# One block of p*v per pair of tiles, and a new timetable for the next pair's preparation and for the weight conversions, in a fused attention, MoE and SwiGLU kernel

## Chip, core and metric

The kernel runs on one core of one Trainium2 chip. The metric is the device time of one execution in microseconds (us); lower is better. The kernel before takes 814.34 us, the median of three runs (813.39 to 814.79).

## What is computed

The reference chains three parts. The part that the change touches is the first, an attention in which a query only sees keys of its own hash bucket:

```python
def _attn_ref(q, k, v, proj):             # q, k, v: (2, 8, 768, 64), proj: (64, 6)
    q_bits = (np.einsum('bhsd,dk->bhsk', q, proj) > 0).astype(np.int64)
    k_bits = (np.einsum('bhsd,dk->bhsk', k, proj) > 0).astype(np.int64)
    powers = 2 ** np.arange(n_bits)
    mask = (q_bits * powers).sum(-1)[:, :, :, None] == (k_bits * powers).sum(-1)[:, :, None, :]
    scores = np.where(mask, scale * np.matmul(q, k.transpose(0, 1, 3, 2)), -1000000000.0)
    attn = np.exp(scores - scores.max(-1, keepdims=True))
    attn = attn / (attn.sum(-1, keepdims=True) + 1e-09)
    return np.matmul(attn, v).astype(np.float32)
```

Its output (1536 tokens of 512) goes through a mixture of 8 experts with 192 tokens each, and then through a normalised SwiGLU layer whose three weights arrive as 64-bit floats.

## The kernel before, in words

**Units.** Heads are worked in pairs: 2 batches by 4 pairs of heads are 8 pairs, numbered p. A pair has 6 tiles of 128 queries, and a tile has two heads, so a pair is 12 *units*, and the main loop (L601) runs over 96 units u. A unit is one head of one tile of 128 queries against all 768 keys. The place of a unit within its pair, 0 to 11, is called its slot here; slot -1 is the last unit of the pair before.

**What a unit issues.** The order on every engine is written out by hand. In unit u:
- `expo(u + 1)` (L346): ScalarE turns the scores of the next unit into exponentials (tile `pr`).
- `transp(u)` (L354): TensorE transposes the six 128x128 blocks of `pr` into two PSUM tiles `m` (three in all, shared with other work); VectorE copies the first out and ScalarE the second, and in every fourth unit ScalarE copies both (L363, L365).
- `scores(u + 2)` (L325): four score matmuls (L336, L339) into one of two PSUM buffers `sc`; VectorE takes the row minimum and two small operations (L341 to L343), which `expo` needs. L339 multiplies the second stack of q and k, which ends in the bucket signs.
- in even units `comb` and `comb_v` (L392, L408): one matmul and the scaling of a finished tile.
- `pv(i, part)` (L368): p*v of tile i, whose units are 2i and 2i+1. The six key blocks are split: blocks 0 to 2 of both heads in unit 2i+2 (part 0), blocks 3 to 5 in unit 2i+3 (part 1), six matmuls each, with weights of 64 columns into one 64-row half of the PSUM tile `xo`. Behind part 1, ScalarE copies `xo` out (L385). `rinv` (L400) stands in odd units.

**Filler.** Behind this, each unit runs the steps that a table `fill` holds for it:
- preparation of pair p+1, at the slots of `SLOTS`: four half transposes of q and k (`prep_t`, L267: TensorE, ScalarE, then two GpSimd operations each, L285 and L286), `prep_d` behind the second half of each (L302: six DMAs that stack the parts), two sign projections (`prep_p`, L288: six matmuls and a VectorE comparison each) and `prep_s` (L315: four DMAs that add the signs `sg` to the stacks). One unit later `load_pair` fetches q, k and v of the pair after (three DMAs).
- 36 conversions of 128x512 weights from 64 to 32 bits (`conv`, L245: one ScalarE, two VectorE and four GpSimd operations), one every 2.4 units from unit 5; each is loaded 5 units ahead into one of three wide buffers (`conv_load`, L239) and stored 3 units later (`conv_store`, L261).

All these DMAs are issued in program order from SP's one queue. Behind the loop come the choice of experts, the experts and the SwiGLU layer, which the change does not touch.

Of the kernel before, what the change touches and what calls it, by code (L numbers as in the profile page):

```python
# [9 lines left out]
F32 = mybir.dt.float32  # L10
# [5 lines left out]
I64 = mybir.dt.int64  # L16
AF = mybir.ActivationFunctionType
# [6 lines left out]
BIG = 2.0 ** 30  # L24
ACT_EVAC = 1
SLOTS1 = (0, 0, 4, 5, 5, 6)
CONV = 5
SLOTS = (-1, 0, 1, 3, 5, 6)
WSTEP = (4, 7, 9, 10, 10, 13, 15, 16)
POOL_LO = (0, 1, 4, 5, 7)  # L30
DVE_HI = (0, 4)
# [15 lines left out]
def lsh_attention__moe__swiglu_kernel(ctx, tc, q, k, v, proj, m_wg, m_w1, m_w2,  # L47
                                      f_wg, f_wv, f_wo, f_g, out):
    nc = tc.nc
# [6 lines left out]
    TPB = S // 128  # L56
# [28 lines left out]
    wk = att.enter_context(tc.tile_pool(name="wk", bufs=2))  # L85
    cv = att.enter_context(tc.tile_pool(name="cv", bufs=2))
    ps_s = att.enter_context(tc.tile_pool(name="ps_s", bufs=2, space=PSUM))
    ps_v = att.enter_context(tc.tile_pool(name="ps_v", bufs=1, space=PSUM))
# [17 lines left out]
    def chunk(p, j):  # L106
        return j if p == 0 else 2 * (j % (TPB // 2)) + j // (TPB // 2)
# [119 lines left out]
    convs = []  # L227
    for src, dst in ((f_wg, wg_d), (f_wv, wv_d), (f_wo, wo_d)):
        n = src.shape[0] * src.shape[1] // (128 * 512)
# [5 lines left out]
    def cv_at(src, i):  # L235
        per = src.shape[1] // 512
        return slice((i // per) * 128, (i // per) * 128 + 128), slice((i % per) * 512, (i % per) * 512 + 512)

    def conv_load(n):  # L239
        src, dst, i = convs[n]  # L240
        w = cv.tile([128, 512], I64, name="w64", bufs=3)
        nc.sync.dma_start(w, src[cv_at(src, i)])
        CV[n] = w

# [78 lines left out]
    SC, PR, PTT, RS, XO = {}, {}, {}, {}, {}  # L323

    def scores(u):  # L325
        i, h = divmod(u, 2)
        p, t = divmod(i, TPB)
        k1, k2 = STK["k", p]
        q1, q2 = STK["q", p]
        if h == 0:  # L330
            RS[i] = wk.tile([128, 2, 4], F32, name="rs", bufs=4)
        rs = RS[i]
        ps = ps_s.tile([128, 2, 512], F32, name="sc")
        qs = slice(place(p, t) * 128, (place(p, t) + 1) * 128)
        for n in range(2):
            nc.tensor.matmul(ps[:, n, :HALF], q1[:, h, qs], k1[:, h, n * HALF:(n + 1) * HALF],  # L336
                             start=True, stop=False)
        for n in range(2):
            nc.tensor.matmul(ps[:, n, :HALF], q2[:64 + NS, h, qs], k2[:64 + NS, h, n * HALF:(n + 1) * HALF],  # L339
                             start=False, stop=True)  # L340
        nc.vector.tensor_reduce(rs[:, h, 0:1], ps[:, :, :HALF], axis=AX.XY, op=OP.min)  # L341
        nc.vector.tensor_scalar(rs[:, h, 1:2], rs[:, h, 0:1], BIG / 2, -1.0, op0=OP.is_lt, op1=OP.mult)
        nc.vector.tensor_scalar(rs[:, h, 2:3], rs[:, h, 0:1], BIG / 2, rs[:, h, 0:1], op0=OP.is_lt, op1=OP.mult)  # L343
        SC[u] = ps

    def expo(u):  # L346
        i, h = divmod(u, 2)
        rs, ps = RS[i], SC.pop(u)
        pt = wk.tile([128, 2, HALF], F32, name="pr", bufs=3)
        nc.scalar.activation(pt, ps[:, :, :HALF], AF.Exp, scale=rs[:, h, 1:2], bias=rs[:, h, 2:3],  # L350
                             accum_out=rs[:, h, 3:4])
        PR[u] = pt

    def transp(u):  # L354
        pt = PR.pop(u).rearrange("p a b -> p (a b)")
        o = wk.tile([128, TPB, 128], F32, name="pt", bufs=4)
        for half in range(2):
            t = ps_m.tile([128, 512], F32, name="m")[:, :HALF].rearrange("p (c k) -> p c k", c=3)
            for i in range(3):
                c = half * 3 + i  # L360
                nc.tensor.transpose(t[:, i, :], pt[:, c * 128:(c + 1) * 128], ident)  # L361
            if half == 1 or u % 4 < ACT_EVAC:
                nc.scalar.activation(o[:, 3 * half:3 * half + 3, :], t, AF.Copy)  # L363
            else:
                nc.vector.tensor_copy(o[:, 0:3, :], t)  # L365
        PTT[u] = o

    def pv(i, part):  # L368
        p = i // TPB
        vt = LD["v", p]  # L370
        if part == 0:
            if i < NU // 2 - 1:
                XO[i] = ps_v.tile([128, 128], F32, name="xo")
            else:
                XO[i] = ps_s.tile([128, 2, 512], F32, name="sc")[:, 0, :128]
        xo = XO[i]
        a = (PTT[2 * i], PTT[2 * i + 1])
        for c in range(3 * part, 3 * part + 3):
            for h in range(2):
                nc.tensor.matmul(xo[64 * h:64 * h + 64], vt[:, h, chunk(p, c), :], a[h][:, c, :],  # L380
                                 start=(c == 0), stop=(c == TPB - 1))
        if part == 1:
            del PTT[2 * i], PTT[2 * i + 1]
            xt = wk.tile([128, 128], F32, name="xt", bufs=3)
            nc.scalar.activation(xt, xo, AF.Copy)  # L385
            XO[i] = xt

    XS = {}

# [2 lines left out]
    def comb(i):  # L392
        p, t = divmod(i, TPB)
        pc = ps_m.tile([128, 512], F32, name="m")
        nc.tensor.matmul(pc[:, :2 * W], XO.pop(i), cb[:, p % HP, :], start=True, stop=True)
        PC[i] = pc
# [3 lines left out]
    def rinv(i):  # L400
        rs = RS.pop(i)
        ri = wk.tile([128, 2, 2], F32, name="ri", bufs=2)
        for h in range(2):
            nc.vector.tensor_scalar(ri[:, h, 0:1], rs[:, h, 3:4], 1e-9, None, op0=OP.add)
        nc.vector.reciprocal(ri[:, :, 1:2], ri[:, :, 0:1])
        RI[i] = ri
# [101 lines left out]
    NU = NPAIR * TPB * 2  # L508
    fill = {}

    def at(u, f, *a):
        fill.setdefault(u, []).append((f, a))

    for p in range(1, NPAIR):
        u0 = (p - 1) * TPB * 2
        slots = iter(SLOTS if p > 1 else SLOTS1)
        for nm in "kq":
            for half in range(2):
                n = u0 + next(slots)
                at(n, prep_t, p, nm, half)  # L520
            at(n, prep_d, p, nm)
        for half in range(2):
            n = u0 + next(slots)
            at(n, prep_p, p, half)
        at(n, prep_s, p)
        if p + 1 < NPAIR:
            at(n + 1, load_pair, p + 1)
    for n in range(len(convs)):
        u = CONV + n * 12 // 5
        at(u - 5, conv_load, n)  # L530
        at(u, conv, n)
        at(u + 3, conv_store, n)
    for i in range(8):
# [59 lines left out]
    for s in range(2):  # L593
        r = slice(64 * s, 64 * s + 64)
# [6 lines left out]
    for u in range(NU + 3):  # L601

        if u + 1 < NU:
            expo(u + 1)
        if u < NU:
            transp(u)
        if u + 2 < NU:
            scores(u + 2)
        if u == NU:
            rinv(u // 2 - 1)  # L610
            pv(u // 2 - 1, 0)
            pv(u // 2 - 1, 1)
        if u % 2 == 0 and u >= 4:
            comb(u // 2 - 2)
            comb_v(u // 2 - 2)
        if u % 2 == 1 and 3 <= u < NU:
            rinv(u // 2 - 1)
        if 2 <= u < NU:
            pv(u // 2 - 1, u % 2)
        for f, a in fill.pop(u, []):  # L620
            f(*a)
    assert not fill
# [690 lines left out]
```

## Time and profile before

| what | value |
|---|---|
| median of three runs | 814.34 us |
| the profiled execution: its own time | 814.53 us |
| its span in the trace | 812.7 us |
| main loop (from the first scores to the last `comb`) | about 15 to 300 us |
| choice of experts, with little TensorE work | about 300 to 345 us |
| experts and SwiGLU | about 345 to 813 us |

Times in the trace count from the start of the span. PE is TensorE's matmul row, whose ends are modelled, PEld its weight loads, DVE is VectorE, ACT ScalarE, POOL GpSimd, and SPq SP's queue of DMA issues. In a timeline the columns are start (us), duration (us), engine, line and operation, output and inputs, and in brackets the idle time before it and what ended that.

### The profile page before, as it was taken

What the parts mean: (1) busy time and instruction counts of PE and PEld (TensorE: products, weight loads), DVE (VectorE), ACT (ScalarE), POOL (GpSimd) and SP (SyncE); (2) the same over time, 40 slices, a digit from 0 to 9 for tenths busy, and PEclk for the clock granted to TensorE, in tenths of its full rate; (3) what the DMA queues carried; (4) which work ended last, traced back from release to release, by engine and by line L of the source; (5) the groups of instructions that cost most, each with busy time, mean ns of one, the idle gap of its engine ahead of it and who ended that gap; (6) DMA issues with size and microseconds to landing.
All of it is one profiled execution on the core that took longest, in us unless ns stands there. A gap on an engine that the chain in (4) does not pass through costs nothing.

```text
span 812.7 us, 14759 instructions
## 1 busy us (share of the span) xinstructions
PE 761.3 (94%) x5317; PEld 685.2 (84%) x5317; DVE 513.7 (63%) x1342; ACT 398.0 (49%) x863; POOL 328.6 (40%) x309
## 2 busy tenths in 40 slices
PE   7999999999989983698999999999999999999997
PEld 3788777787878863498999999999999999999996
DVE  7788786889878878467787887766422332233222
ACT  3677765676766762265676776644211221121111
POOL 3278786877868720586767660000100010001001
PEclk8999999999999995699999999999999999999999
DMA  3578897989879612377777834363200110001001
GB/s 79 175 206 217 258 248 208 271 253 278 213 233 268 192 34 78 96 226 226 244 255 241 261 102 156 117 195 117 78 1 1 40 39 1 1 1 40 1 1 39
DMA packets 89770, 115.58 MB, mean 142 GB/s; under 512 B 22124, under 2 KB 68188, under 8 KB 89692
## 3 DMA queue, kind: packets, MB, share of 16 engines
q1 hardware_dynamic: 87612, 108.28, 44.8%
q0 software_dynamic: 1920, 6.29, 2.1%
q8 instruction: 44, 0.72, 0.4%
q14 instruction: 34, 0.28, 0.1%
q10 hardware_dynamic: 160, 0.00, 0.0%
HBM read 77.62 MB, written 18.87 MB: 119 GB/s over the span
## 4 chain that ended last, share of the span: by engine, by line
PE 37%; issue 18%; POOL 1%; DVE 1%; ACT 1%; POOLq 0%; ACTq 0%; DVEq 0%
PE pg L1194 6%; PE pv L1194 6%; PE py L1029 6%; PE po L1222 6%; PE ph L1005 6%; PE py L1031 3%; PE ph L1007 3%; POOL out_dram L1230 1%; PE ph L983 1%; PE py L1101 0%; DVE wl L218 0%; PE px L1061 0%; PE px L1084 0%; ACT bt L1015 0%; DVE yn L1091 0%
## 5 line engine op out<-in xcount | busy, mean ns | idle before, releaser
L1230 POOL DMA_INDIRECT out_dram<-ot,oi x12 | 11.7, 974 | 307.8 <-DVE ot L1228 306.2
L350 ACT ACTIVATE pr<-sc,rs 128x768 f32<-128x768 f32 x96 | 94.9, 989 | 50.4 <-DVE rs L343 31.6
L341 DVE TENSOR_REDUCE rs<-sc 128x1 f32<-128x768 f32 x96 | 91.5, 953 | 34.7 <-PE sc L339 34.2
L218 POOL TENSOR_TENSOR wl<-wr,wh 128x1024 fp32r<-128x1024 f32 x39 | 95.0, 2446 | 44.0 <-PE ph L983 20.9
L1203 DVE TENSOR_TENSOR a<-sg,pg 128x384 f32<-128x384 f32 x48 | 26.6, 553 | 103.1 <-ACT sg L1201 103.1
L361 PE MATMUL m<-ident,pr 128*128 128x128 f32 x576 | 83.4, 281 | 3.1 <-ACT pt L363 2.5
L380 PE MATMUL xo<-pt,ld_v 128*64 128x128 f32 x1128 | 82.9, 282 | 0.0
L1005 PE MATMUL ph<-xg,wh 128*128 128x384 f32 x256 | 75.3, 363 | 3.8 <-DVE ht L1022 3.1
L1029 PE MATMUL py<-ht,wh 128*128 128x384 f32 x256 | 76.7, 364 | 0.0
L361 PEld LDWEIGHTS m<-ident,pr 128*128 128x128 f32 x576 | 63.8, 141 | 15.1 <-issue 7.4
L380 PEld LDWEIGHTS xo<-pt,ld_v 128*64 128x64 f32 x1128 | 60.0, 137 | 18.6 <-issue 11.9
L1201 ACT ACTIVATE sg<-pg 128x384 f32<-128x384 f32 x48 | 23.5, 490 | 105.8 <-PE pg L1194 105.7
L1207 ACT ACTIVATE ah<-a 128x384 fp32r<-128x384 f32 x48 | 25.2, 525 | 99.3 <-DVE a L1204 99.3
L1194 PE MATMUL pg<-xh,gl 128*128 128x384 f32 x192 | 64.6, 336 | 0.0
L1194 PE MATMUL pg<-xl,gh 128*128 128x384 f32 x192 | 64.5, 336 | 0.0
L1194 PE MATMUL pg<-xh,gh 128*128 128x384 f32 x192 | 64.5, 336 | 0.0
L1194 PE MATMUL pv<-xh,vl 128*128 128x384 f32 x192 | 64.4, 335 | 0.0
L1194 PE MATMUL pv<-xl,vh 128*128 128x384 f32 x192 | 64.4, 335 | 0.0
L1194 PE MATMUL pv<-xh,vh 128*128 128x384 f32 x192 | 64.4, 335 | 0.0
L1031 PE MATMUL py<-ht,wl 128*128 128x192 f32 x256 | 63.7, 253 | 0.0
L215 ACT ACTIVATE wh<-wr 128x1024 fp32r<-128x1024 f32 x50 | 51.2, 1054 | 14.2 <-PE py L1029 11.4
L339 PE MATMUL sc<-s_k,s_q 82*128 82x384 f32 x192 | 49.9, 341 | 8.7 <-DMA s_q<-sg 8.7
(252 smaller groups left out, 1952.4 us busy)
## 6 DMA issues: line engine op xcount, KB each, us to landing
wr<-in_moe_w_dram SPq DMA_DIRECT2D x64, 512.0 KB, 4.7
w<-in_moe_w_gate_dram SPq DMA_DIRECT2D x12, 512.0 KB, 6.4
w<-in_moe_w_val_dram SPq DMA_DIRECT2D x12, 512.0 KB, 5.7
w<-in_moe_w_out_dram SPq DMA_DIRECT2D x12, 512.0 KB, 5.3
s_k<-nh_k SPq DMA_DIRECT2D x28, 192.0 KB, 3.4
s_q<-nh_q SPq DMA_DIRECT2D x28, 192.0 KB, 4.2
ld_v<-in_v_dram SPq DMA_DIRECT2D x8, 384.0 KB, 6.2
wg_d<-ha SPq DMA_DIRECT2D x12, 256.0 KB, 5.5
```

The source lines that it names most:

```text
L215: nc.scalar.activation(WH[i], WR[i], AF.Copy)
L218: (nc.gpsimd if pool else nc.vector).tensor_tensor(WL[i], WR.pop(i), WH[i], op=OP.subtract)
L339: nc.tensor.matmul(ps[:, n, :HALF], q2[:64 + NS, h, qs], k2[:64 + NS, h, n * HALF:(n + 1) * HALF], start=False, stop=True)
L341: nc.vector.tensor_reduce(rs[:, h, 0:1], ps[:, :, :HALF], axis=AX.XY, op=OP.min)
L350: nc.scalar.activation(pt, ps[:, :, :HALF], AF.Exp, scale=rs[:, h, 1:2], bias=rs[:, h, 2:3], accum_out=rs[:, h, 3:4])
L361: nc.tensor.transpose(t[:, i, :], pt[:, c * 128:(c + 1) * 128], ident)
L380: nc.tensor.matmul(xo[64 * h:64 * h + 64], vt[:, h, chunk(p, c), :], a[h][:, c, :], start=(c == 0), stop=(c == TPB - 1))
L1005: hi = lambda: nc.tensor.matmul(ph[:, :2 * CAP], wh[:, d], xg[:, d].rearrange("p a b -> p (a b)"), start=(d == 0), stop=(d == KD - 1), ski ...
L1029: hi = lambda: nc.tensor.matmul(py[d][:, :2 * CAP], wh[:, ds], ht[:, f].rearrange("p a b -> p (a b)"), start=(f == 0), stop=(f == KF - 1), ...
L1031: lo = lambda: nc.tensor.matmul(py[d][:, :CAP], wl[:, ds], ht[:, f, 0], start=False, stop=False, skip_group_check=True)
L1194: nc.tensor.matmul(t[:, :TJ], a[:, d, :], b_[:, d, :], start=(n == 0), stop=(n == 3 * KD - 1))
L1222: nc.tensor.matmul(PO[j][t], a[:, ts], b_, start=(f == 0 and n == 0), stop=(f == KG - 1 and n == 2))
```

## The change

`SLOTS` of pairs from the second on becomes (-1, 0, 1, 2, 4, 5): the last half transpose of q moves from slot 3 to 2, the two sign projections from 5 and 6 to 4 and 5, with them `prep_s` to 5 and the next `load_pair` to 6. The conversions get a timetable for each of the 8 pairs, two units apart in all but the last: 4 in the first pair, then 4, 5, 4, 5, 4, 4 and 6 (before: 3, then 5 in each of the next six, and 3). The wide buffers become four, and the loads of slots 3 to 7 are all put two units before their pair begins, unless the buffer is still in use. p*v of a tile becomes one block of twelve matmuls in the even unit, `rinv` stands behind it, and the copy of `xo` stands in the odd unit right behind `expo`.

```diff
-CONV = 5
-SLOTS = (-1, 0, 1, 3, 5, 6)
+CONV1 = (5, 7, 9, 11)
+CONV5 = (2, 4, 6, 8, 10)
+CONV4 = (3, 5, 7, 9)
+CONVN = (0, 2, 4, 5, 7, 9)
+SLOTS = (-1, 0, 1, 2, 4, 5)
...
-        w = cv.tile([128, 512], I64, name="w64", bufs=3)
+        w = cv.tile([128, 512], I64, name="w64", bufs=4)
...
-    def pv(i, part):
+    def pv(i):
...
-        for c in range(3 * part, 3 * part + 3):
+        a = (PTT.pop(2 * i), PTT.pop(2 * i + 1))
+        for c in range(TPB):
             for h in range(2):
                 nc.tensor.matmul(xo[64 * h:64 * h + 64], vt[:, h, chunk(p, c), :], a[h][:, c, :],
                                  start=(c == 0), stop=(c == TPB - 1))
-        if part == 1:
-            del PTT[2 * i], PTT[2 * i + 1]
-            xt = wk.tile([128, 128], F32, name="xt", bufs=3)
-            nc.scalar.activation(xt, xo, AF.Copy)
-            XO[i] = xt
+
+    def pv_out(i):
+        xt = wk.tile([128, 128], F32, name="xt", bufs=3)
+        nc.scalar.activation(xt, XO[i], AF.Copy)
+        XO[i] = xt
...
-    for n in range(len(convs)):
-        u = CONV + n * 12 // 5
-        at(u - 5, conv_load, n)
+    turns = [CONV1, CONV4, CONV5, CONV4, CONV5, CONV4, CONV4, CONVN]
+    units = [w * TPB * 2 + u for w, t in enumerate(turns) for u in t]
+    for n, u in enumerate(units):
+        r = u % (TPB * 2)
+        at(max(u - r - 2 if 3 <= r < 8 else u - 5, units[n - 4] + 1 if n > 3 else 0), conv_load, n)
         at(u, conv, n)
         at(u + 3, conv_store, n)
...
         if u + 1 < NU:
             expo(u + 1)
+        if u % 2 == 1 and 3 <= u <= NU + 1:
+            pv_out(u // 2 - 1)
         if u < NU:
             transp(u)
         if u + 2 < NU:
             scores(u + 2)
-        if u == NU:
-            rinv(u // 2 - 1)
-            pv(u // 2 - 1, 0)
-            pv(u // 2 - 1, 1)
         if u % 2 == 0 and u >= 4:
             comb(u // 2 - 2)
             comb_v(u // 2 - 2)
-        if u % 2 == 1 and 3 <= u < NU:
+        if u % 2 == 0 and 2 <= u <= NU:
+            pv(u // 2 - 1)
             rinv(u // 2 - 1)
-        if 2 <= u < NU:
-            pv(u // 2 - 1, u % 2)
```

How the rows stand before and after the change is shown at three places; lines from L28 on have other numbers in the changed kernel (L361 is L364 there, L380 is L382, L253 is L256, L310 is L313, L320 is L323).

TensorE, two units without filler, first an odd one and then an even one (`xo` is p*v, `m<-ident,pr` the transposes, `sc` the scores, `m<-cb,xt` comb). Before:

```order
L361 MATMUL m<-ident,pr 128x128 x6
L336 MATMUL sc<-s_k,s_q 128x384 x2
L339 MATMUL sc<-s_k,s_q 128x384 x2
L380 MATMUL xo<-pt,ld_v 64x128 x6
L361 MATMUL m<-ident,pr 128x128 x6
L336 MATMUL sc<-s_k,s_q 128x384 x2
L339 MATMUL sc<-s_k,s_q 128x384 x2
L395 MATMUL m<-cb,xt 128x144
L380 MATMUL xo<-pt,ld_v 64x128 x6
```

And now:

```order
L364 MATMUL m<-ident,pr 128x128 x6
L339 MATMUL sc<-s_k,s_q 128x384 x2
L342 MATMUL sc<-s_k,s_q 128x384 x2
L364 MATMUL m<-ident,pr 128x128 x6
L339 MATMUL sc<-s_k,s_q 128x384 x2
L342 MATMUL sc<-s_k,s_q 128x384 x2
L397 MATMUL m<-cb,xt 128x144
L382 MATMUL xo<-pt,ld_v 64x128 x12
```

The odd unit's p*v has gone behind the even unit's, and in the odd unit the next transposes follow the scores directly.

VectorE around a conversion in an odd unit (`rs` are the three score operations, `ri` is `rinv`, `ha` and `sg` the conversion, `pt` the copy of transposes). Before:

```order
L341 TENSOR_REDUCE rs<-sc 128x1
L342 TENSOR_SCALAR rs<-rs 128x1
L343 TENSOR_SCALAR rs<-rs 128x1
L404 TENSOR_SCALAR ri<-rs 128x1 x2
L405 RECIPROCAL ri<-ri 128x2
L253 TENSOR_SCALAR ha<-w_2673 128x512
L254 TENSOR_SCALAR sg<-w_2673 128x512
```

And now:

```order
L344 TENSOR_REDUCE rs<-sc 128x1
L345 TENSOR_SCALAR rs<-rs 128x1
L346 TENSOR_SCALAR rs<-rs 128x1
L256 TENSOR_SCALAR ha<-w_1851 128x512
L257 TENSOR_SCALAR sg<-w_1851 128x512
L344 TENSOR_REDUCE rs<-sc 128x1
```

`rinv` has left the odd unit; the conversion still stands between the scores' operations of the odd unit and those of the even unit behind it.

SP's queue around `prep_s` of one pair (`s_q<-nh_q` and `s_q<-nl_q` are `prep_d`, `s_k<-sg` and `s_q<-sg` are `prep_s`, `w` a conversion's load, `wv_d` a conversion's store, `wr` an expert's weights, `ld_` the load of the next pair). Before:

```order
L310 DMA s_q<-nh_q 64x2x384
L311 DMA s_q<-nh_q 64x2x384
L312 DMA s_q<-nl_q 64x2x384
L263 DMA wv_d<-ha 128x512
L242 DMA w_2126<-in_moe_w_val_dram 128x512
L263 DMA wv_d<-ha 128x512
L320 DMA s_k<-sg 18x2x384 x2
L320 DMA s_q<-sg 18x2x384 x2
L98 DMA ld_k<-in_k_dram 128x2x384
```

And now:

```order
L313 DMA s_q<-nh_q 64x2x384
L314 DMA s_q<-nh_q 64x2x384
L315 DMA s_q<-nl_q 64x2x384
L205 DMA wr<-in_moe_w_dram 128x4x256
L245 DMA w_2131<-in_moe_w_val_dram 128x512
L323 DMA s_k<-sg 18x2x384 x2
L323 DMA s_q<-sg 18x2x384 x2
L101 DMA ld_k<-in_k_dram 128x2x384
```

Between `prep_d` of q and `prep_s` a store and another store stood beside a load; now there is no store, but a load and an expert's weights.

## Rows read from the trace of the kernel before

**Rows 1.** Page, part 1 (busy, share, instructions) and rows of part 2 (40 slices).

```profile
PE 761.3 (94%) x5317; PEld 685.2 (84%) x5317; DVE 513.7 (63%) x1342; ACT 398.0 (49%) x863; POOL 328.6 (40%) x309
...
PEclk8999999999999995699999999999999999999999
DMA  3578897989879612377777834363200110001001
```

**Rows 2.** Stretches of the loop: start:end, length, busy us by engine, clock, DMA share, GB/s.

```profile
15.20:52.40 37.20, 35.20 (x271) 28.39 (x271) 28.98 (x75) 23.95 (x54) 14.62 (x16) 1.00 0.55 156
...
82.98:118.06 35.08, 33.19 (x302) 28.17 (x301) 28.18 (x81) 24.48 (x55) 27.68 (x30) 1.00 0.88 256
...
257.92:287.44 29.52, 29.43 (x278) 24.70 (x277) 25.73 (x82) 21.98 (x50) 21.01 (x21) 1.00 0.61 189
```

**Rows 3.** Timeline, two units without filler, TensorE's weight loads.

```profile
286.84 0.64 PEld L361 LDWEIGHTS m<-ident,pr 128*128 128x128 f32 x6 [0.17 <-issue]
...
287.44 0.30 PEld L336 LDWEIGHTS sc<-s_k,s_q 128*128 128x128 f32 x2
...
287.73 0.36 PEld L339 LDWEIGHTS sc<-s_k,s_q 82*128 82x128 f32 x2
...
288.34 0.64 PEld L380 LDWEIGHTS xo<-pt,ld_v 128*64 128x64 f32 x12 [0.25 <-issue]
...
289.15 0.64 PEld L361 LDWEIGHTS m<-ident,pr 128*128 128x128 f32 x6 [0.17 <-ACT pt L363]
...
290.04 0.36 PEld L339 LDWEIGHTS sc<-s_k,s_q 82*128 82x128 f32 x2
...
290.39 0.36 PEld L395 LDWEIGHTS m<-cb,xt 128*128 128x128 f32 x2
...
290.90 0.63 PEld L380 LDWEIGHTS xo<-pt,ld_v 128*64 128x64 f32 x12
291.70 0.64 PEld L361 LDWEIGHTS m<-ident,pr 128*128 128x128 f32 x6 [0.17 <-ACT pt L363]
```

**Rows 4.** Waits, 0 to 340 us: who for what, total us, times, longest.

```profile
ACT xt L385 <- PE xo L380: 25.6, 40, 1.4
...
PEld xo L380 <- issue: 11.9, 48, 0.3
...
PE sc L339 <- DMA s_q<-sg: 8.7, 4, 3.0
```

**Rows 5.** Timeline around one change of pairs, SP's queue and TensorE.

```profile
76.66 0.78 SPq L312 DMA_DIRECT2D s_q<-nl_q  x1
...
77.77 0.68 DVE L297 TENSOR_SCALAR sg<-m,pm 114x384 fp32r<-114x384 f32 x1 [0.44 <-PE m L294]
...
80.32 1.70 SPq L320 DMA_DIRECT2D s_k<-sg  x2
...
82.08 1.60 SPq L320 DMA_DIRECT2D s_q<-sg  x2
...
87.38 0.59 PE L339 MATMUL sc<-s_k,s_q 82*128 82x384 f32 x2 [1.47 <-DMA s_q<-sg]
```

**Rows 6.** Stretches around the wait at 121 to 124 us, columns as in rows 2.

```profile
118.00:122.00 4.00, 3.00 (x28) 2.25 (x25) 3.29 (x10) 3.47 (x8) 3.39 (x5) 1.00 0.99 251
122.00:126.00 4.00, 2.13 (x17) 1.69 (x17) 1.45 (x4) 0.20 (x2) 3.53 (x3) 0.85 1.08 307
126.00:130.00 4.00, 4.00 (x30) 3.58 (x29) 1.88 (x6) 1.80 (x5) 0.00 (x0) 0.72 0.88 346
```

**Rows 7.** Timeline, the chain of one unit on VectorE and ScalarE, and a conversion before it.

```profile
285.09 0.42 DVE L253 TENSOR_SCALAR ha<-w 128x512 int32<-128x512 int32 x1
...
285.77 0.55 DVE L365 COPY pt<-m 128x384 f32<-128x384 f32 x1
...
286.23 0.95 DVE L341 TENSOR_REDUCE rs<-sc 128x1 f32<-128x768 f32 x1
...
288.45 0.96 DVE L341 TENSOR_REDUCE rs<-sc 128x1 f32<-128x768 f32 x1
...
289.51 0.20 DVE L343 TENSOR_SCALAR rs<-rs 128x1 f32<-128x1 f32 x1
289.63 0.20 DVE L404 TENSOR_SCALAR ri<-rs 128x1 f32<-128x1 f32 x2
289.81 0.99 ACT L350 ACTIVATE pr<-sc,rs 128x768 f32<-128x768 f32 x1 [0.27 <-DVE ri L404]
...
290.80 0.86 ACT L363 ACTIVATE pt<-m 128x384 f32<-128x384 f32 x2
```

More of the change, by code (lines that the diff above doesn't have):

```diff
@@ L366, in transp @@
         PTT[u] = o
-    def pv(i, part):
+    def pv(i):
         p = i // TPB
         vt = LD["v", p]
[L371 to L375, printed above, removed]
+        if i < NU // 2 - 1:
+            XO[i] = ps_v.tile([128, 128], F32, name="xo")
+        else:
+            XO[i] = ps_s.tile([128, 2, 512], F32, name="sc")[:, 0, :128]
         xo = XO[i]
-        a = (PTT[2 * i], PTT[2 * i + 1])
-        for c in range(3 * part, 3 * part + 3):
+        a = (PTT.pop(2 * i), PTT.pop(2 * i + 1))
+        for c in range(TPB):
             for h in range(2):
@@ L527, in lsh_attention__moe__swiglu_kernel @@
             at(n + 1, load_pair, p + 1)
-    for n in range(len(convs)):
-        u = CONV + n * 12 // 5
-        at(u - 5, conv_load, n)
+    turns = [CONV1, CONV4, CONV5, CONV4, CONV5, CONV4, CONV4, CONVN]
+    units = [w * TPB * 2 + u for w, t in enumerate(turns) for u in t]
+    assert len(units) == len(convs)
+    for n, u in enumerate(units):
+        r = u % (TPB * 2)
+        at(max(u - r - 2 if 3 <= r < 8 else u - 5, units[n - 4] + 1 if n > 3 else 0), conv_load, n)
         at(u, conv, n)
```

## The prediction, as put on record before the run

> **What bounds the kernel now.** I read the busy times first: over the span TensorE's matmul row is busy 94%, its weight loads 84%, every other engine 63% or less [rows 1]. The change only touches the loop, so I went to stretches of it. In the last pair, which prepares nothing, the matmul row fills 29.43 of 29.52 us and VectorE 25.73; in a pair with preparation and five conversions 33.19 of 35.08, with VectorE and GpSimd at about 28 [rows 2]. So TensorE sets the pace, and the weight-load row, at 24.70 of 29.52 us, leaves room that the matmul row hides. The Trainium skill (Perfetto Trace Analysis, section Identifying the Most-Contended Engine) says that matmul busy time is a poor measure of how full TensorE is, and that the busy share of weight loads is a better one; by the first row the last pair could gain 0.09 us, by the second up to 4.8.
>
> Where the weight loads rest is seen in two units without filler [rows 3]. An odd unit goes 286.84 to 289.15, an even one 289.15 to 291.70: 2.31 and 2.55 us, 4.86 a tile. In the odd unit there are two holes around p*v: 0.25 us before it and 0.17 behind it; in the even unit 0.15 (290.39 + 0.36 to 290.90) and 0.17. Between transposes, scores and comb there is none. The hole of 0.25 is there 48 times [rows 4], for nothing that the profile shows ("issue"). It depends on p*v alone: what stands behind p*v may be transposes that waited for nothing or for ScalarE, and the hole is 0.17 both times. The Trainium skill (TensorEngine Tiling (Array Packing), section Key Properties) says that a change of tiling mode drains TensorE; p*v is the one step here with 64-column weights, so the trace agrees with it, but does not prove it.
>
> The second loss is at changes of pairs. Four of the seven times the score matmul waits for the sign rows, 8.7 us in all, 3.0 at most [rows 4]. At one of them [rows 5] the signs are ready at 78.45 (77.77 + 0.68), but the queue of SP is still busy with what stands before, since `prep_d` of q was issued as late as 76.66; the sign DMAs go out from 80.32 to 83.68, and the matmul that needs them starts at 87.38 after 1.47 us of waiting. After another such wait the granted clock falls: 0.85 and 0.72 in 122 to 130 us [rows 6], part of it at 1.2 GHz and the rest at 2.4, which costs about 4 x 0.15 + 4 x 0.28 = 1.7 us.
>
> **The change part by part.**
>
> *p*v in one block.* The same twelve matmuls, so their own time stays (0.64 + 0.63 us), but of four holes per tile two go: 0.25 + 0.17 = 0.42 us. The even unit is then 2.55 + 0.63 = 3.18 us, the odd one 2.31 - 0.42 - 0.64 = 1.25, together 4.43 for 4.86. 47 of 48 tiles were split: 19.7 us. In the first pair, 37.2 us long with weight loads busy 28.39 [rows 2], TensorE mostly waits for the start-up, so I take nothing for four of its tiles, 1.7 us: **18.0 us gained.** The bounds are 0 (if another engine paces the loop) and 19.7.
>
> *Preparation one slot earlier.* The GpSimd halves of q now stand before the conversions, so `prep_d` of q is issued by slot 3, and SP is free when the signs come, one slot earlier too. What is left to land: from the end of the projections in slot 5 to the matmul in slot 10 are four units, 2 x 4.43, and 0.6 + 0.3 of the unit itself, 9.8 us. Of it the comparison takes 0.44 + 0.68, and four issues 3.36 (80.32 to 83.68), which leaves 5.3 us to land. In rows 5 the last issue started about 82.88 and had landed at 87.38: at most 4.5. So it fits with about 0.8 us to spare, with fewer transfers in front of it. **8.7 us gained** and with it the clock, **1.7 us**. Bounds: 0 and 10.4.
>
> *`rinv` and the copy of `xo`.* ScalarE's wait for p*v, 25.6 us in all [rows 4], goes, since the copy now comes a unit later. ScalarE is busy 22 to 24 us in a pair [rows 2], so this is worth nothing by itself. The PSUM tile is written again only 1.25 + 1.75 us after the block's end, and the copy stands right behind `expo`.
>
> *The new wait.* Without p*v behind the odd unit's scores, the chain from scores to their transposes has less cover. That chain is [rows 3, 7]: the scores' weights end at 288.09 (287.73 + 0.36), the reduction starts 0.36 later at 288.45, its last small operation ends at 289.71, `expo` runs from 289.81 to 290.80: 2.71 us. The transposes that need it start at 291.70, so 3.61 us were there and 0.90 spare. After the change there are 3.61 - 0.42 = 3.19, for either kind of unit: **0.48 us spare.** A conversion takes 0.68 us of VectorE (285.09 to 285.77) and a copy of transposes 0.46 (285.77 to 286.23) [rows 7]. In an odd unit VectorE ends the scores' operations 0.36 + 1.26 = 1.62 us after the scores, then converts until 2.30 and copies until 2.76, while the even unit's scores want it at 1.25 + 0.36 = 1.61: late by 1.15, or by 0.69 where ScalarE does the copy. Less the 0.48 spare, TensorE stops for 0.67 or 0.21 us, 0.44 in the mean. Of 23 conversions in odd slots, those in slot 3 (4) and in slot 5 with projections behind (5) have over 1 us of projections as cover; 14 are left: 6.2 us. In even units the conversion has p*v as cover and costs nothing. Where ScalarE copies both halves its copies end 0.86 us after `expo`, at 3.57 after the scores, and the odd unit's second three transposes want that buffer at 3.19 + 0.32 = 3.51: 0.1 us in 24 units, with the step to TensorE, 2.4 us. **8.6 us lost.** Bounds: 0, if neighbouring units take up each delay, and all 18.0, if each tile loses its 0.42. I take the worked-out value; it is near the middle.
>
> *Conversions and loads.* Their work is the same, 36 of each. Pairs with preparation have four or five in place of five; three more go to the last pair, whose GpSimd is busy 21.0 of 29.5 us with five in that stretch [rows 2]: a sixth, 4 us, still fits. The loads stand further ahead, and SP issues as many. Cost: nothing, covered by two units or more. If that cover is gone ScalarE, which converts in order, holds up `expo`; that is the slower rival.
>
> *The end.* The last tile's p*v was one block already, and its copy and comb follow as before: 0.
>
> **Sum**, against the profiled execution's own time of 814.5 us (its span of 812.7 and 1.8 around it; the median of the runs is 814.3): 814.5 - 18.0 - 8.7 - 1.7 + 8.6 = **794.7 us.**
>
> **The rivals.**
> - *No new wait shows*: delays are taken up by the units with filler. For it speaks that VectorE's work in a pair, 28 us, is under the new length of about 31. 814.5 - 28.4 = 786.1. Chance 0.12.
> - *VectorE's chain paces every tile*, and p*v in one block gives nothing. For it speak the 0.48 us of spare and VectorE's 25.73 us in a pair that would last 6 x 4.43 = 26.6 us [rows 2]; against it that a pair with preparation has more room. 814.5 - 10.4 = 804.1. Chance 0.15.
> - *The changes of pairs still wait*, since shorter units come nearer to the landing and the DMA share, 0.88 of 35 us [rows 2], is 31 us of work for a pair of about 31. 814.5 - 18.0 + 8.6 = 805.1. Chance 0.12.
> - *The change doesn't do what it says*: the holes belong to the count of p*v matmuls, or a new hole appears between scores and transposes, which never stood side by side here. Then 804.1 as well. Chance 0.05. The last two losses together: 814.5, chance 0.02.
> - *Slower*: three loads of 512 KB now go out together two units before a pair, ahead of `prep_d`. At 256 GB/s [rows 2] that is 6.1 us of transfers, and the DMA engines were already full around the waits (0.99, 1.08) [rows 6]. If signs need over 5.3 us to land, TensorE waits at all seven changes. With 3.0 us more than now in each and the clock's 1.7 behind it: 7 x (3.0 + 1.7) = 33 us, less 9.4 from the blocks: 814.5 + 33 - 9.4 + 0 = 838. It costs more than it gains from about 1.4 us each on (9.4 / 7). Against it: the loads are three units ahead of `prep_d` of q and seven ahead of the signs. Chance 0.05.
>
> **How the numbers follow.** My forecast, 794.7, has the rest, 0.49. The range reaches from the case without a new wait to those in which one of the gains fails: 786 to 806, leaving out the slower case, the case of no gain, and a little on each side. A measurement of this kernel can tell about 0.2% (1.6 us) from no change: faster by more than that 0.93, within it 0.02, slower 0.05.
>
> **What would show it.** In two units without filler: an odd unit of about 1.25 us, an even one of 3.2, no 0.25 hole before p*v of an odd unit, and no hole between scores and transposes. No wait of L342 (L339 before) for the sign rows, and a clock of 1.00 in all of the loop. Weight loads idle on VectorE or ScalarE, in units behind a conversion in slots 7 and 9 above all, 6 to 11 us in all. The loop some 20 us shorter, and nothing changed in length behind it. I am wrong if the tile stays at 4.86 us, if waits for DMA remain, or if ScalarE waits for the loads of weights.

## Result, and the profile after

The changed kernel takes 801.66 us in the median of four runs (799.88 to 802.12), beside 813.87 us (813.26 to 814.79) for the kernel before: a ratio of 0.9845, with an interval of 0.9826 to 0.9864. It is 12.2 us faster. The forecast was 19.8 us faster, at 794.7; the time lies in the range and 7.0 us above the point. The profiled execution took 799.88 us with a span of 798.0.

The page of the changed kernel, parts 1 and 2, answers to [rows 1]:

```profile
PE 750.5 (94%) x5317; PEld 686.4 (86%) x5317; DVE 509.3 (64%) x1342; ACT 394.7 (49%) x863; POOL 329.1 (41%) x309
...
PEclk9999999999999975799999999999999999999999
DMA  3577899987879321577877823563100110000001
```

TensorE's matmul row lost 10.8 us of busy time, the weight loads none: the same loads fit into a shorter span. The slices with a lower clock (7, 5, 7) begin at 14 x 20 = 280 us, behind the loop, where the experts are chosen and TensorE has little to do.

Three stretches of the loop, columns as in [rows 2]: two pairs with preparation and the last pair, each from its first scores on.

```profile
51.90:84.29 32.39, 31.92 (x303) 28.50 (x302) 27.56 (x82) 23.93 (x54) 27.81 (x30) 1.00 0.81 239
117.87:149.54 31.67, 31.47 (x303) 28.52 (x301) 26.32 (x86) 23.72 (x54) 25.10 (x28) 1.00 0.93 267
249.41:278.40 28.99, 27.11 (x268) 23.72 (x267) 27.05 (x78) 21.02 (x47) 24.16 (x24) 1.00 0.56 186
```

The granted clock is now 1.00 in all of them, also in the pair that begins at 117.87, where it had fallen [rows 6]. In the last pair the matmul row fills 27.11 of 28.99 us, where it filled 29.43 of 29.52 [rows 2]: now TensorE waits there. VectorE, with 27.05, is as busy as the matmul row.

Who waits for what in the seven pairs from 52 to 278 us (us in total, times, longest):

```profile
DVE rs L344 <- PE sc L342: 19.0, 44, 1.1
PEld m L364 <- ACT pr L353: 9.1, 17, 1.1
...
PEld m L364 <- ACT pt L366: 4.2, 21, 0.2
PEld m L364 <- issue: 3.9, 10, 1.9
...
PE sc L342 <- DMA s_q<-sg: 0.3, 1, 0.3
```

The wait of the scores for the sign rows, 8.7 us in [rows 4], is down to 0.3. In its place the weight loads of the transposes wait for ScalarE's `expo` (L353): 9.1 us. VectorE (`rs`) itself waits 19.0 us for scores, so in pairs with preparation its busy time is not what paces the loop.

Units without filler, TensorE's weight loads, to be held against [rows 3]:

```profile
247.44 0.64 PEld L364 LDWEIGHTS m<-ident,pr 128*128 128x128 f32 x6 [0.17 <-ACT pt L366]
248.04 0.30 PEld L339 LDWEIGHTS sc<-s_k,s_q 128*128 128x128 f32 x2
248.33 0.37 PEld L342 LDWEIGHTS sc<-s_k,s_q 82*128 82x128 f32 x2
248.78 0.66 PEld L364 LDWEIGHTS m<-ident,pr 128*128 128x128 f32 x6
249.41 0.30 PEld L339 LDWEIGHTS sc<-s_k,s_q 128*128 128x128 f32 x2
249.70 0.36 PEld L342 LDWEIGHTS sc<-s_k,s_q 82*128 82x128 f32 x2
250.05 0.36 PEld L397 LDWEIGHTS m<-cb,xt 128*128 128x128 f32 x2
250.55 1.29 PEld L382 LDWEIGHTS xo<-pt,ld_v 128*64 128x64 f32 x24
252.01 0.64 PEld L364 LDWEIGHTS m<-ident,pr 128*128 128x128 f32 x6 [0.17 <-ACT pt L366]
```

The two holes of the odd unit, 0.25 and 0.17, are gone. The odd unit goes from one first score load to the next, 248.04 to 249.41: 1.37 us, and 1.35 to 1.43 in other units of its kind. The even one is 3.20 to 3.22. That is 4.57 a tile, where 4.43 was forecast and 4.86 stood before.

For what follows I give each unit by the interval between the first score load (L339) of one unit and that of the next, numbered k0 to k11 within a pair, all read from the timeline. From the first scores of the loop to the last it was 277.1 us and is 263.25, that is 13.9 less; from the last scores to the end 520.4 and 519.6. So nearly all of the gain of this trace, 13.9 of 14.7 us, is in the loop.

### The profile page after: what moved, and what is told of

The parts are those of the page before. It is cut to its first block, busy times and chain, and to the rows that moved or that the text cites. A ratio compares the mean times of both kernels' runs of the same rounds, so it can differ in the third digit from the quotient of the medians.

```text
span 798.0 us, 14720 instructions
## 1 busy us (share of the span) xinstructions
PE 750.5 (94%) x5317; PEld 686.4 (86%) x5317; DVE 509.3 (64%) x1342; ACT 394.7 (49%) x863; POOL 329.1 (41%) x309
## 4 chain that ended last, share of the span: by engine, by line
PE 37%; issue 18%; DVE 1%; POOL 1%; ACT 1%; POOLq 0%; ACTq 0%; DVEq 0%
PE pg L1198 6%; PE pv L1198 6%; PE py L1033 6%; PE po L1226 6%; PE ph L1009 5%; PE py L1035 3%; PE ph L1011 3%; POOL out_dram L1234 1%; PE ph L987 1%; PE py L1105 0%; DVE wl L221 0%; PE px L1065 0%; PE px L1088 0%; ACT bt L1019 0%; ACT sq L1051 0%
## 5 line engine op out<-in xcount | busy, mean ns | idle before, releaser
L1234 POOL DMA_INDIRECT out_dram<-ot,oi x12 | 11.7, 977 | 307.7 <-DVE ot L1232 306.2
L353 ACT ACTIVATE pr<-sc,rs 128x768 f32<-128x768 f32 x96 | 95.3, 992 | 54.5 <-DVE rs L346 22.6
L344 DVE TENSOR_REDUCE rs<-sc 128x1 f32<-128x768 f32 x96 | 91.5, 953 | 23.8 <-PE sc L342 23.4
L364 PE MATMUL m<-ident,pr 128*128 128x128 f32 x576 | 83.9, 279 | 8.9 <-DVE pt L368 4.1
L364 PEld LDWEIGHTS m<-ident,pr 128*128 128x128 f32 x576 | 63.3, 140 | 23.8 <-ACT pr L353 10.1
L382 PE MATMUL xo<-pt,ld_v 128*64 128x128 f32 x1128 | 72.0, 277 | 0.0
L382 PEld LDWEIGHTS xo<-pt,ld_v 128*64 128x64 f32 x1128 | 60.6, 137 | 6.9 <-issue 0.2
L366 ACT ACTIVATE pt<-m 128x384 f32<-128x384 f32 x120 | 56.0, 489 | 6.6 <-PE m L364 6.5
L218 ACT ACTIVATE wh<-wr 128x1024 fp32r<-128x1024 f32 x50 | 51.2, 1053 | 13.7 <-PE py L1033 11.4
```

What stands on the lines that cost most here:

```text
L218: nc.scalar.activation(WH[i], WR[i], AF.Copy)
```

## The experiments

**One part of the change at a time.** `block_only` keeps the old timetable, slots and three wide buffers and takes p*v in one block, with `rinv` and the copy of `xo` where the change puts them. `timetable_only` is the other half. `changed_again` is the changed kernel once more beside them.

```diff
 block_only, against the kernel before
-        for c in range(3 * part, 3 * part + 3):
+        for c in range(TPB):
...
 timetable_only, against the changed kernel
-    def pv(i):
+    def pv(i, part):
...
-        if u % 2 == 0 and 2 <= u <= NU:
-            pv(u // 2 - 1)
+        if 2 <= u < NU:
+            pv(u // 2 - 1, u % 2)
```

> Only p*v in one block (with its copy and rinv); preparation, conversions and loads as before. Theory (in the changed kernel the block's gain is mostly given back: ScalarE's copy of a prepared half waits for the long block and holds up the next expo, and conversions in odd units make VectorE late): the same happens here and the waits for sign rows at changes of pairs stay, so 808 to 812 us, 2 to 6 under before. Rival (the block is worth its 18 us, and the new timetable costs): 796 to 799 us.

> Only the timetable: preparation, conversions, loads and four buffers as in the changed kernel, p*v in two halves as before. Theory: the waits for sign rows (8.7 us) and the low clock behind one of them (1.7) go and nothing else, 803 to 805 us, 10 under before. Rival (the timetable costs what the block gains): 808 us or more, with new waits of TensorE for ScalarE and VectorE.

> The changed kernel once more, beside the others on one chip: 800 to 802 us by every theory. Where its trace differs from the first by 1 to 2 us, waits for sign rows and a lower clock at a change of pairs would be the difference; a difference elsewhere speaks against the claim that these waits are gone.

| kernel | median, us | ratio to before, interval | first to last scores, us |
|---|---|---|---|
| block_only | 819.92 | 1.0042 (1.0003 to 1.0081) | 284.2 |
| timetable_only | 801.91 | 0.9806 (0.9760 to 0.9852) | 264.0 |
| changed_again | 801.51 | 0.9803 (0.9756 to 0.9849) | 263.3 |

In this series the kernel before itself ran from 810.4 to 821.8 us (13 runs), so ratios have wide intervals; the medians of the three kernels of one series are held against each other. The timetable alone gives as much as the whole change, 1 us more than its theory allowed. The block alone gains nothing: by its ratio it is 0.4% slower, with an interval that ends just short of no change, where its two expectations were 2 to 6 us under the kernel before, or the full 18. Its waits say where the gain goes (0 to 340 us):

```profile
PE sc L339 <- DMA s_q<-sg: 16.6, 6, 5.2
...
PEld m L361 <- ACT pr L350: 7.8, 15, 0.7
...
PEld sc L339 <- DMA ld_q<-in_q_dram: 5.5, 1, 5.5
```

and the clock around two of the changes of pairs (columns as in [rows 2]):

```profile
84.00:93.00 9.00, 7.35 (x55) 6.55 (x55) 5.50 (x15) 4.70 (x11) 6.08 (x6) 0.81 0.95 301
229.00:243.00 14.00, 8.78 (x58) 7.83 (x57) 5.95 (x15) 4.97 (x11) 6.16 (x7) 0.76 0.81 260
```

With shorter units and the same DMAs the score matmul comes to the sign rows sooner, and part of what the block saves is waited there: 16.6 us for 8.7, six changes of pairs for four, with the granted clock at 0.76 to 0.81, so part of the time at 1.2 GHz. The 5.5 us of the weight loads are one of the same six waits, the longest, with another DMA named, and don't add to the 16.6. The first interval of a pair was 5.4 to 11.1 us there, against 3.2 without a wait. The transposes wait for ScalarE's `expo` as well, 7.8 us: k3 and k5, each 1.69 us without waits under the old slots, are 2.55 and 2.16 in every pair with preparation, 8.0 us in six pairs. How the loss divides between the two, no run shows.

In `timetable_only` the weight loads of p*v still wait as before (lines view, 15 to 288 us: busy, mean ns, idle before):

```profile
L383 PEld LDWEIGHTS xo<-pt,ld_v 128*64 128x64 f32 x1128 | 59.6, 136 | 18.6 <-issue 12.0
```

In the changed kernel that idle time is

```profile
L382 PEld LDWEIGHTS xo<-pt,ld_v 128*64 128x64 f32 x1128 | 60.6, 137 | 6.9 <-issue 0.2
```

so the block saves 11.7 us of idle time there, and it must be given back elsewhere. The same view has it: the transposes' loads waited 13.7 us with the timetable alone, and

```profile
L364 PEld LDWEIGHTS m<-ident,pr 128*128 128x128 f32 x576 | 63.3, 140 | 23.8 <-ACT pr L353 10.1 <-ACT pt L366 4.4 <-issue 4.3
```

23.8 with the block too: 10.1 more, most of it for `expo`.

**What the hole is.** `wide_pv` is the kernel before with p*v's weights 128 columns wide instead of 64: each matmul takes 64 columns of the neighbouring head's v along, and their products are thrown away, so nothing is left out and p*v costs more; ScalarE copies the two heads' halves apart.

```diff
...
-                nc.tensor.matmul(xo[64 * h:64 * h + 64], vt[:, h, chunk(p, c), :], a[h][:, c, :],
+                at_ = (h * TPB + chunk(p, c)) * D - 64 * h
+                nc.tensor.matmul(xo[:, h], vt.rearrange("p h c d -> p (h c d)")[:, at_:at_ + 128], a[h][:, c, :],
...
```

> The kernel before, with p*v weights of 128 columns instead of 64 (the neighbouring head's columns come along and are thrown away), so that all of TensorE's work has weights of 128 columns; twelve matmuls per tile in two halves as before. If the holes around p*v (0.25 us before, 0.17 behind) come from the change between weights of 64 and of 128 columns, both are gone (below 0.05 us). If they come from the number of matmuls or from the p*v step itself, they stay. The time is longer by every theory, 830 us or more, since the weight loads of p*v double.

It took 835.16 us (one run), with these weight loads in an even and an odd unit of the last pair:

```profile
280.83 0.36 PEld L398 LDWEIGHTS m<-cb,xt 128*128 128x128 f32 x2
281.13 1.43 PEld L381 LDWEIGHTS xo<-pt,ld_v 128*128 128x128 f32 x12
282.48 0.69 PEld L361 LDWEIGHTS m<-ident,pr 128*128 128x128 f32 x6
...
283.42 0.37 PEld L339 LDWEIGHTS sc<-s_k,s_q 82*128 82x128 f32 x2
283.78 1.48 PEld L381 LDWEIGHTS xo<-pt,ld_v 128*128 128x128 f32 x12
285.17 0.36 PEld L361 LDWEIGHTS m<-ident,pr 128*128 128x128 f32 x3
```

No hole is left, before p*v or behind it: it comes with the step from 128 to 64 columns and back. (With 64 columns each matmul also writes one 64-row half of `xo`; the two go together here, and no run separates them.) The Trainium skill (TensorEngine Tiling (Array Packing), section Key Properties) says that a change of tiling mode drains TensorE; these runs agree, and price it: 0.25 us going in behind scores, 0.17 coming out. `wide_pv` has a second use. Its units are longer (5.65 a tile), its DMAs are those of before, and no scores wait for sign rows. So with one timetable the waits for them are 0 at 5.65 us a tile, 8.7 at 4.86 and 16.6 at 4.57. That agrees with a landing that sets a time of its own, to which units only come sooner or later; it is no fixed time, for from the end of the last issue to the scores it is 3.6 to 4.9 us at the four waits of the kernel before and 2.8 to 5.8 at the six of `block_only`.

**Where the new waits are.** In the changed kernel k3 is 1.99 us in every pair with preparation, and k5 is 1.78, or 2.33 where a conversion stands in slot 2; a unit without waits would be 1.69 (it has a half transpose in it) and 1.36. VectorE and ScalarE before k3's transposes:

```profile
64.21 1.29 PEld L382 LDWEIGHTS xo<-pt,ld_v 128*64 128x64 f32 x24
...
65.13 0.20 DVE L346 TENSOR_SCALAR rs<-rs 128x1 f32<-128x1 f32 x1
...
65.67 0.55 PE L281 MATMUL m<-ident,ld_q 128*128 128x128 f32 x3
...
66.25 0.49 ACT L285 ACTIVATE nr_q<-m 128x384 f32<-128x384 f32 x1 [1.35 <-PE m L281]
...
66.64 0.99 ACT L353 ACTIVATE pr<-sc,rs 128x768 f32<-128x768 f32 x1
...
67.77 0.64 PEld L364 LDWEIGHTS m<-ident,pr 128*128 128x128 f32 x6 [0.51 <-ACT pr L353]
```

The row minimum (`rs`) that `expo` needs is there at 65.33. But ScalarE's next instruction is the copy of the half transpose, which stands behind the block of twelve on TensorE, and so waits 1.35 us, until 66.25. `expo` is queued behind it, starts at 66.64 and the next transposes stop for 0.51 us. The theory was then that this order costs some 5 us; the rival, that VectorE's conversions make the waits. `copy_behind_expo` issues that copy, and `prep_d`, behind the `expo` of the next unit, in even units from the second pair on. `even_convs` leaves the order and puts the conversions of all odd slots into even ones. `keys_late` moves the scaling and comparison of the first batch's keys, which VectorE does beside a conversion just ahead of the sixth pair (its k1 is 3.55), by seven units. `all_three` has all of it, with the conversions' ScalarE step behind `expo` as well.

```diff
 copy_behind_expo, against the changed kernel
...
             expo(u + 1)
+        while LATER:
+            LATER.pop(0)()
...
+            if u % 2 == 0 and u >= 12 and f is prep_t:
+                f(*a, True)
+            elif u % 2 == 0 and u >= 12 and f in (prep_d,):
+                LATER.append(lambda f=f, a=a: f(*a))
 even_convs, against the changed kernel
-CONV1 = (5, 7, 9, 11)
+CONV1 = (4, 6, 8, 10)
-CONV4 = (3, 5, 7, 9)
-CONVN = (0, 2, 4, 5, 7, 9)
+CONV4 = (4, 6, 8, 10)
+CONVN = (0, 2, 4, 6, 8, 10)
 keys_late, against the changed kernel
-    at(HP * TPB * 2 + 9, key_scale)
-    at(HP * TPB * 2 + 10, keys, 0)
+    at(HP * TPB * 2 + 16, key_scale)
+    at(HP * TPB * 2 + 17, keys, 0)
 all_three, against copy_behind_expo: the edits of the other two, and
-            elif u % 2 == 0 and u >= 12 and f in (prep_d,):
+            elif u % 2 == 0 and u >= 12 and f in (prep_d, conv):
```

> The changed kernel; in even units ScalarE's copy of a prepared half (and prep_d behind it) is issued after the next unit's expo instead of before it, from the second pair on. Theory (this copy waits for the block of p*v and holds up expo): the waits of 0.3 to 0.6 us at slots 1 and 3 go, 12 of them, 4 to 6 us: 795 to 798 us. Rival (VectorE's conversions in odd units are all of the loss): 800 to 802 us, no change.

> The changed kernel with all conversions in even units (slots 4, 6, 8, 10, in the last pair 0, 2, 4, 6, 8, 10). Theory: the wait of 0.8 us behind the conversion in slot 9 goes in five pairs, and part of the last pair's, 4 to 6 us: 795 to 798 us, less what ScalarE's part of a conversion costs when it stands ahead of expo in an even unit. Rival (the copies of the preparation are all of the loss): 800 to 802 us.

> The changed kernel with two VectorE steps of the first batch (the scale of the keys and the keys, units 57 and 58) moved to units 64 and 65, where the sign projections keep TensorE busy. Theory (in the trace TensorE waits 0.6 and 1.7 us behind them): 2 us less, 799 to 800 us. Rival (the wait moves with them): no change.

> The three edits together, and ScalarE's part of a conversion in an even unit also behind the next expo. Theory: their gains add, 790 to 793 us, and the tile comes near 4.43 us without filler. Rival (another engine or the DMA paces the loop at about the present length): 796 us or more.

| kernel | median, us | ratio to before, interval | k3 | k5 | k1 | last pair |
|---|---|---|---|---|---|---|
| changed kernel | 801.66 | 0.9845 (0.9826 to 0.9864) | 1.99 | 1.78, 2.33 | 2.40 | 29.03 |
| copy_behind_expo | 796.59 | 0.9771 (0.9723 to 0.9818) | 1.69 | 1.36 | 2.40 | 29.02 |
| even_convs | 803.47 | 0.9873 (0.9823 to 0.9922) | 1.99 | 1.78, 2.33 | 1.69 | 27.40 |
| keys_late | 801.00 | 0.9828 (0.9781 to 0.9875) | 1.99 | 1.78, 2.33 | 2.40 | 29.03 |
| all_three | 805.98 | 0.9898 (0.9850 to 0.9947) | 1.69 | 1.36 | 1.69 to 2.24 | 28.46 |

Intervals are those of the profiled executions; k1 is that behind a conversion that stands in slot 9 in the changed kernel. `copy_behind_expo` does what the theory says, 4.4 us below `keys_late` of the same series, which stands where the changed kernel does. In its timeline `expo` comes first and the transposes don't wait:

```profile
64.36 0.20 DVE L358 TENSOR_SCALAR rs<-rs 128x1 f32<-128x1 f32 x1
...
64.69 0.99 ACT L365 ACTIVATE pr<-sc,rs 128x768 f32<-128x768 f32 x1 [0.28 <-DVE rs L358]
...
65.67 0.48 ACT L297 ACTIVATE nr_q<-m 128x384 f32<-128x384 f32 x1
...
66.47 0.75 PEld L376 LDWEIGHTS m<-ident,pr 128*128 128x128 f32 x6
```

Of the 5.4 us in k3 and k5 a part comes back: 1.39 us ahead of the second score matmuls at one change of pairs (149.5), for which the profile names nothing, and 1.3 us as a wait for a load of k.

`even_convs` missed. It does mend k1 and the last pair, so the conversion in an odd slot is what costs there; but k11 rose from 1.37 to 1.86, since ScalarE's step of a conversion in slot 8 then stands ahead of an `expo`, and the first pair became 2.7 us longer. Over half of that is again an order in a queue: GpSimd now takes up the conversion of slot 4 ahead of the halves of q, and the sign projections wait 0.70 and 0.78 us for these (45.56 and 46.64). `keys_late` missed as well: k1 of the sixth pair fell from 3.55 to 2.10, and behind it k6 rose from 4.31 to 4.97 and k9 from 1.43 to 2.70. The work was only moved. `all_three` missed most, and is slower than `copy_behind_expo` alone: k3 and k5 are mended in it, but its first pair is nearly as long as in `even_convs` (39.1 us for 39.4), and changes of pairs wait again (k0 is 4.5 to 4.8 at three). Here are its TensorE and ScalarE at 151 us:

```profile
151.29 0.68 ACT L253 ACTIVATE lr<-w 128x512 int32<-128x512 uint32 x1 [1.16 <-DMA w<-in_moe_w_val_dram]
...
152.57 0.43 PEld L376 LDWEIGHTS m<-ident,pr 128*128 128x128 f32 x3 [2.00 <-ACT pt L378]
152.99 0.55 PEld L351 LDWEIGHTS sc<-s_k,s_q 128*128 128x128 f32 x2
```

ScalarE's step of the conversion waits for its load, now ahead of the copies that TensorE needs, and behind the wait of 2.00 us the score loads take 0.55 in place of 0.30: the granted clock is 0.53 from 152.5 to 156 us, so nearly all of it at 1.2 GHz. In this stretch it is the same queue, by another instruction; the 9.4 us between the two kernels as a whole are not accounted for.

**Both mended, and the block's worth again.** `copy_and_slots` adds to `copy_behind_expo` only those slots that had paid; `copy_slots_keys` moves the keys too; `copy_slots_split` is `copy_and_slots` with p*v split, and `rinv` and the copy of `xo` placed, as before.

```diff
 copy_and_slots, against copy_behind_expo
-CONV4 = (3, 5, 7, 9)
-CONVN = (0, 2, 4, 5, 7, 9)
+CONV4 = (3, 5, 7, 10)
+CONVN = (0, 2, 4, 6, 8, 10)
```

> The kernel with the half's copy behind the next expo, and three conversions moved: the one of slot 9 to slot 10 in the pairs with four, and the last pair's to 0, 2, 4, 6, 8, 10. Theory (behind a conversion in slot 9 TensorE waits 0.7 us in the next pair's first odd unit, and the last pair's uneven slots cost 1.6): 4 waits of 0.7 and 1.6 us less, 791 to 794 us. Rival (the moved conversions only move the wait): 796 to 798 us.

> The same, with the keys of the first batch in units 64 and 65. Theory: the 1.9 us wait at the keys is partly covered by the sign projections, 1 us less than without, 790 to 793 us. Rival: the same as without, since they then meet a conversion in slot 5.

> The first of these kernels with p*v in two halves again. What is left of the block's worth once the waits are mended is the difference between the two. Theory (two holes of 0.42 us per tile, 18 us, less what conversions and copies still cost): the split kernel takes 799 to 802 us, 6 to 9 more than the block. Rival (the block is worth nothing, whatever the order): the same time within 1 us.

| kernel | median, us | ratio to before, interval | first to last scores, us |
|---|---|---|---|
| copy_and_slots | 794.41 | 0.9749 (0.9712 to 0.9786) | 254.9 |
| copy_slots_keys | 794.30 | 0.9742 (0.9709 to 0.9776) | 256.8 |
| copy_slots_split | 799.99 | 0.9816 (0.9783 to 0.9850) | 262.9 |

`copy_and_slots`, 0.4 us above what its theory allowed, beats both kernels: 21.5 us under the kernel before of its own series (815.95), and, across series, some 7 us under the changed kernel. With the queues mended the block is worth 5.6 us (799.99 - 794.41), a little less than the 6 to 9 expected, where with the timetable of the change it was worth 0.4 (801.91 - 801.51), less than the runs of either kernel scatter. The loads of the transposes now wait

```profile
L376 PEld LDWEIGHTS m<-ident,pr 128*128 128x128 f32 x576 | 64.2, 140 | 14.2 <-ACT pr L365 4.0 <-issue 3.4 <-ACT pt L378 3.4
```

14.2 us for 23.8. Moving the keys gives nothing here either: the rival held.

## Why the prediction was right in sign and short in size

| term | forecast, us | found, us | from |
|---|---|---|---|
| p*v in one block, 43 tiles | -18.0 | -12.5 | 4.57 a tile for 4.86 |
| waits for sign rows | -8.7 | -8.1 | k0 is 3.2 in all pairs but one, which has 0.6 more |
| the clock behind them | -1.7 | -1.7 | taken over, not measured apart; the clock is 1.00 from 15 to 280 us |
| the timetable otherwise | 0 | -3.7 | 32.74 for 33.35 in pairs without such a wait, 6 times |
| new waits | +8.6 | +13.2 | below |
| sum | -19.8 | -12.8 | loop of the profiled run -13.9, medians -12.2 |

**The preparation one slot earlier: right.** The sign rows land in time at six of seven changes. The landing was bounded by 4.5 us, with room for 5.3. That bound was read at one change only: read in the same way, the other three waits of the kernel before give 5.1, 4.4 and 5.7 us, and the last is more than the room, so that it fitted is in part luck. In the one wait that is left the last issue ends at 83.34 and the scores start at 85.24:

```profile
81.75 1.59 SPq L323 DMA_DIRECT2D s_q<-sg  x2
...
85.24 0.59 PE L342 MATMUL sc<-s_k,s_q 82*128 82x384 f32 x2 [0.33 <-DMA s_q<-sg]
```

By intervals the gain is somewhat larger than the two rows of the table: before the change k0 of all pairs, and k1 of the fourth pair, stood 12.1 us above their like, now 0.6. That would bring the sum to some -14.5, beside 13.9 for the loop of the trace.

**p*v in one block: the mechanism right, the size a third too large.** The holes went as forecast, and the even unit is 3.21 for 3.18. The step that failed is "the odd one 2.31 - 0.42 - 0.64 = 1.25": it is 1.37. Of the rest, 0.08 is a gap that now stands between scores and transposes (248.33 + 0.37 to 248.78), which the rival of a new hole had named at 0.42; the remainder is small differences in the loads. What makes the gap stays open.

**The new waits: mis-sized, and mostly of another source.** The step that failed counted conversions in odd slots (14 of them, 6.2 us) and ScalarE's double copies (2.4) and nothing else. Found, as excess over 3.21, 1.36 and 1.69 us in the intervals:

- 5.4 us: ScalarE's copy of the halves prepared in slots 0 and 2, k3 and k5 of six pairs (0.3 x 6, and 0.42 x 4 + 0.97 x 2). `copy_behind_expo` takes it away. The forecast had written "the copy stands right behind `expo`" of another copy, and had called conversions and the preparation covered without asking what the twelve matmuls do to ScalarE's order.
- 3.1 us: conversions in slot 9 with VectorE's own copy behind them, 0.7 each (0.12 where a sign wait hid it). Worked out were 0.67, so this part of the step was good; at slot 7, worked out as 0.21, nothing is seen. The chain of one such unit is that of the forecast:

```profile
150.38 0.72 DVE L256 TENSOR_SCALAR ha<-w 128x512 int32<-128x512 int32 x1
151.02 0.43 DVE L257 TENSOR_SCALAR sg<-w 128x512 int32<-128x512 int32 x1
...
151.36 0.56 DVE L368 COPY pt<-m 128x384 f32<-128x384 f32 x1
...
151.82 0.95 DVE L344 TENSOR_REDUCE rs<-sc 128x1 f32<-128x768 f32 x1
...
154.45 0.74 PEld L364 LDWEIGHTS m<-ident,pr 128*128 128x128 f32 x6 [0.62 <-ACT xt L387]
```

  The conversion and the copy hold up the reduction to 151.82, and TensorE's transposes stop for 0.62 at 154.45. The name in the bracket is the last of a row of waits.
- 1.4 us: conversions in slots 6 and 8 of two pairs, which were to cost nothing as their units are even: 0.2 in k8, whose cause stays open, and 0.5 in k11, where ScalarE's step stands ahead of `expo` (at 115.55, and the transposes stop for 0.60 at 117.27).
- 2.1 us: the last pair with six conversions, two of them in slots 4 and 5. "A sixth, 4 us, still fits" was true of GpSimd, and the wrong engine to ask: VectorE is busy 27.05 of 28.99 us there. With slot 9 the last pair stood 2.9 above its like (29.03 for 6 x 3.21 + 5 x 1.36 = 26.1), and `copy_and_slots` took 1.6 of it.
- 1.2 us: the keys. k1 of the sixth pair is 3.55, 1.86 above its like, of which the timetable alone has 1.1; and k11 ahead of it is 2.26, where `keys_late` has 1.88.

Of ScalarE's double copies, 2.4 us in the forecast, nothing is seen: units that have one and no filler are as long as their like within 0.1 us. That 8.6 and 13.2 are no further apart is in part luck, for over half of what was found comes from sources that the forecast had at nothing.

**The timetable otherwise** gained 3.7 us that the forecast put at nothing. Most is one wait: in each of six pairs of the kernel before the transposes of one unit waited 0.66 to 0.68 us for ScalarE's copy, where 0.17 is usual, with the old slots of preparation and conversions; `timetable_only` has no such wait. The first of them:

```profile
70.41 0.69 PEld L361 LDWEIGHTS m<-ident,pr 128*128 128x128 f32 x6 [0.68 <-ACT pt L363]
```

**The rivals.** The time nearest to 801.66 is 804.1, the rival in which VectorE's chain takes the block's gain, and the net is close to it: the block's 12.5 us are given back as 13.2. Its mechanism is not what happened, for units without filler did get shorter, and about half of what was given back (5.4 + 1.0 of 13.2) hangs on the order in ScalarE's queue and not on VectorE. The slower rival did not come for the new timetable; its mechanism, a landing that is too late, is part of what takes the gain from `block_only`. Working the sum as independent terms hid that: the block is worth 5.6 us with the queues mended, 0.4, within the scatter, with the timetable of the change, and nothing without it (819.92 for 815.75).

The weight-load row was the better guide to room, as the Trainium skill (Perfetto Trace Analysis, section Identifying the Most-Contended Engine) says and the forecast used. By the matmul row the last pair had 0.09 us of room [rows 2], and yet a tile without filler went from 4.86 to 4.57 us. The last pair as a whole did not gain in any run: its eleven intervals were 27.2 us and are 29.0 with six conversions for three; 26.1, its length with today's units and no waits, is only worked out.

## What to carry to other kernels

When the work between two steps of the pacing engine grows or shrinks, walk down the queue of every engine that serves it, instruction by instruction: a copy that waits for the lengthened block, ahead of the one instruction the pacing engine needs, costs more than any busy share shows. Here a saving in the units was worth nothing before the transfers they run into came sooner as well, so move the transfers first and measure the saving on top. A gap's saving is what is left after the next wait: price it against the spare of the chain behind it for each kind of unit, and not only where that chain was known to be tight.

## What was not expected of the hardware

- The hole at a change between 128 and 64 columns of weights has two sizes, 0.25 us in behind scores and 0.17 out, and there is none with 128 columns throughout.
- How steeply the waits for landing grow as units shorten: 0, 8.7 and 16.6 us at 5.65, 4.86 and 4.57 us a tile, with the same DMAs in the same order.
- A wait of 2.0 us at 150 us in `all_three` was followed by a granted clock of 0.53 (152.5 to 156 us) and score loads at 0.55 for 0.30 us; a wait of 1.9 us in the changed kernel (189.7) was not: the clock stays at 1.00 and the score loads behind it take 0.30.
- The wait at one change of pairs scatters between executions. k0 of the third pair is 3.79 us in the changed kernel, 3.67 in `changed_again` and 5.08 in `keys_late`, whose program is the same until far behind it. So 1 to 1.5 us between two single traces need not be the work of an edit.
- The kernel before scattered more in the later series (807.7 to 821.8 us) than in the first (813.3 to 814.8), and the changed one did not. Why stays open.
